# An identity matmul in place of four mask products, in a windowed attention and MLP kernel on one Trainium2 core

## The chip, the cores and the metric

The kernel runs on 1 core of one Trainium2 chip. A core has five engines with an instruction queue each: TensorE (matmul, PE in the views; its weight loads are shown apart as PEld), VectorE (DVE), ScalarE (ACT), GpSimd (POOL) and SyncE (SP). Each engine takes its own instructions strictly in the order in which they are written, and waits where one needs another engine's result or a transfer. SP, ACT and POOL also issue the transfers (DMA) between memory and the core.

The metric is the device time of one execution in microseconds (us), as a median of several runs.

## What is computed

Attention with a causal window of 128 positions plus four "sink" positions that every query sees, and behind it a two-layer MLP with a quick GELU:

```
scores = q @ k.T / sqrt(64)                      # 4 batches, 8 heads, 768 positions, 64 wide
keep   = (key position < 4) | (0 <= query - key < 128)
a      = softmax(where(keep, scores, -1e9))
x      = (a @ v) as 3072 tokens x 512
h      = x @ w_in                                # 512 x 2048
out    = (h * sigmoid(1.702 * h)) @ w_out        # 2048 x 512
```

All inputs and the output are 32-bit floats in memory; the kernel computes in 16-bit floats with 32-bit sums.

## The kernel before

**Blocks.** The 3072 tokens are cut into 12 blocks `k` of 256 tokens, three (`r` = 0, 1, 2) to a batch. A block has four pairs `p` of heads. For each pair: the queries and keys are cast to 16 bits and transposed on TensorE (`tp`, L547) and copied to `qkT`; the scores are multiplied (`s`, L671) into two banks of PSUM, one for each head; ScalarE takes the exp (L700) into `at`; VectorE multiplies `at` by the 0/1 tile `mask` (L710 for `r` > 0, 512 columns a head; L714 for `r` = 0, 384 columns a head); TensorE multiplies by v (`av`, L742 and L747), with a column of ones that gives the sums; VectorE takes the reciprocal (L762) and the product `xn` (L764); TensorE transposes `xn` (`xt`, L775) and a copy gives `xT`. In blocks with `r` > 0 the sink keys come in through a matmul and an exp of their own (`sink`, L576, and L584), from the small tiles `ks16` and `vs16`, into which the first keys and values of the batch are copied (`ks`, L567 by way of L304; `vs`, L470). In blocks 0 and 1 the scores are made one pair at a time, later for two pairs at once, with transposes of other blocks behind them.

**The MLP.** Block k's `xT` is multiplied with `w_in` in eight slabs `s` (`mm1`, L815), each two sums over four parts of 256 columns; ScalarE takes tanh (L829), VectorE joins it to `gT` (L831). The second layer (`mm2`) is plain for block 0 (L993) and takes seven products in place of eight for the others (L892), with sums of operands on VectorE (L862) and partial results added up on VectorE (L919).

**The order.** No loop fixes the order of the instructions. The kernel describes its work as operations with dependences, a cost on each engine that may do it, and a rank (`prio`); a small planner (`Plan.run`) then places them one after the other in a planned time, with planned landings of the transfers, and the instructions of each engine are written in that order. What changes a cost, a rank, a dependence or a choice of engine can therefore reorder every queue after it. The planner also fills TensorE's planned idle time before 12 us with dummy matmuls of `zero` (L1061). Rank and engines are set by constants: `EARLY` shifts a block's attention ahead in eighths of a block's time, `VS_ON`/`VS_AT` and `KS_ON` say which engines may make the `vs` and `ks` copies of batch 0 and when, `LOADS` ranks the first transfers on POOL's queue.

**The loads.** Block 0's queries and keys come in through SP and ACT as 32-bit floats (L497). Block 1's come through SP (L509), in two halves of the heads, and are cast by whichever engine the planner picks (L524). All others, v and the weights are cast on the way by transfers that POOL issues (L426, L450, L386). POOL's queue has eight places: an issue waits until the transfer eight places before has landed. `w_in`'s first two slices of 512 columns come in two halves each.

**The lines that matter here.** The helper `copy` is L304, so every copy and cast of every engine has that line, and tiles tell them apart. `scores` starts at L648, its mask products at L707; `back`, with `av`, at L722; `weights` at L373.

Of the kernel before, what the change touches and what calls it, by code (L numbers as in the profile page):

```python
# [14 lines left out]
P = 128  # L15
# [39 lines left out]
class Plan:  # L55
# [4 lines left out]
    def op(self, eng, dur, lat, fn, deps=(), prio=0.0, acq=None, rel=(), kind=""):  # L60
        return self.any({eng: (dur, lat)}, lambda _: fn(), deps, prio, acq, rel, kind)
# [143 lines left out]
def kernel(  # L205
# [26 lines left out]

    SEVEN_FROM, SEVEN_TO = 1, NK

    EARLY = {1: 5, 2: 5, 3: 0}
    HALVES_FROM, HALVES_X_FROM = 4, 3
    V1_BEHIND = None

# [1 line left out]

    ROUNDED_FROM = 2, 2
    GO1 = None, 1
    VS_ON, VS_AT = "POOL DVE ACT", 15000.0
    QK_NS, V_NS = 1000, 300
    NH = NF // 2
    HM = d_model // 2
# [6 lines left out]

    ident = pool.tile([P, P], FP16, name="ident")
    mask = pool.tile([P, 4 * P], FP16, name="mask")
    dummy = pool.tile([P, 8], FP16, name="dummy")
    zero = pool.tile([P, P], FP16, name="zero")
    w_in16 = pool.tile([P, 4, d_ff], FP16, name="w_in16")
# [26 lines left out]
    def f32(o, i=0):  # L285
        return bank[o.banks[i]]
# [7 lines left out]
    def pick(ns, engs):  # L294
        return {e: ns[e] for e in engs.split()}
# [12 lines left out]
    def uses(name, slot, o):  # L308
        users.setdefault((name, slot), []).append(o)
# [3 lines left out]
        return users.pop((name, slot), [])  # L313

    NEVER = -1e9
    o_zero = op("DVE", 100, 200, lambda: nc.vector.memset(zero, 0.0), prio=NEVER, kind="const")

    def make_ident():
# [20 lines left out]
    o_mask0 = op("POOL", 1900, 1950, make_mask, [o_mask1], prio=NEVER + 1, kind="const")  # L339
    o_mask = op("DVE", 560, 660, keep_sinks, [o_mask0], prio=NEVER + 3.5, kind="const")  # L340

    def ones():
        for t in v16:
            nc.vector.memset(t[:, :, :, D : D + 1], 1.0)
# [17 lines left out]

    COPY = ["DVE ACT"] * NK

    KS_ON = "POOL DVE ACT", "POOL"

    ISSUE = 700
    o_win, o_wout, o_w = {}, {}, []
# [4 lines left out]
    def weights(j, at):  # L373

        if j < 4:
            dst, src = w_in16[:, :, bass.ts(j, 512)], moe_w_in[:, bass.ts(j, 512)]
        else:
            dst, src = w_out16[:, bass.ts(j - 4, 4)], moe_w_out[bass.ts(j - 4, 512), :]

        before = o_w[-3:-2]  # L380
        parts = 2 if j < HALVED else 1
        got = []
        for n in range(parts):
            c = slice(4 * n // parts, 4 * (n + 1) // parts)
            def f(c=c):
                nc.gpsimd.dma_start(dst[:, c], src.rearrange("(c p) f -> p c f", p=P)[:, c])  # L386
            o_l = op("POOL", ISSUE - 150 * (parts - 1), (2600 / parts,), f, before, prio=load_at(f"w{j}b") if n and f"w{j}b" in LOADS else at + 0.1 * n, kind="w")
            loads.append(o_l)
            got += [o_l] * (2 // parts)
        o_w.append(o_l)  # L390
        for n in range(2):
            (o_win if j < 4 else o_wout)[2 * (j % 4) + n] = got if j < 4 else o_l

    L = 16600.0
    LOADS = ["a0", "a1", "v0", "b1", "v1", "w0", "w1", "a2", "w2", "a2", "w3", "v2", "w4", "w6", "w5", "w7"]

    SLABS = (0, 1, 4, 5, 2, 3, 6, 7)

    def load_at(x):
# [128 lines left out]

    k_ap = k

    o_qkT, o_ks, o_se, o_m, o_xT, o_n = {}, {}, {}, {}, {}, {}

    def front(k, p):

# [7 lines left out]
        if k < HALVES_FROM:  # L542
            def tp():
                ps = f16(o_tp).rearrange("d (e j i p) -> d e j i p", e=2, j=2, i=2)
                for i in range(2):
                    for e in range(2):
                        nc.tensor.transpose(  # L547
                            ps[:, e, :, i, :], c16[:, i, e, 2 * p : 2 * p + 2].rearrange("s h d -> s (h d)"), ident
                        )

            if p == 0:
                o_T["war", k] = reuse("qkT", k % RKT)
            war = o_T["war", k]
            o_tp = op("PE", 4 * pe_ns(P), 3 * pe_ns(P) + P / 2.4 + 166, tp,
                      [*o_cqk[k, p], o_ident] + war, prio=base - 5 * h8, acq=("t", 1), kind="tp")
            uses("qk16", k % RQ, o_tp)
            o_cp = plan.any(pick({"DVE": (331, 430), "ACT": (477, 600)}, COPY[k]), lambda e: copy(
                e, T[:, :, :, p].rearrange("d j e s -> d e j s"),
                f16(o_tp).rearrange("d (e j s) -> d e j s", e=2, j=2)),
                [o_tp] + war, prio=base - 5 * h8, rel=[(o_tp, 0)], kind="cp")  # L560
            o_qkT[k, p] = [o_cp]
# [86 lines left out]
    def scores(k, pairs, more=None):  # L648
# [6 lines left out]
        for p in pairs:  # L655
            u = NP * k + p
            o_m["war", k, p] = reuse("at", u % RA)
            deps += [*o_qkT[k, p]] + o_m["war", k, p] + ([*o_qkT[k - 1, p]] if r else [])

        def s():  # L660
            for n, p in enumerate(pairs):
                T, prev = qkT[k % RKT], qkT[(k - 1) % RKT]
                if r:
                    parts = [(prev, 1, PREV, 0, 1), (T, 0, CUR0, 0, 2), (T, 1, CUR1, 1, 2)]
                else:
                    parts = [(T, 0, 0, 0, 2), (T, 1, 2 * P, 1, 2)]
# [13 lines left out]
        if more:  # L680
# [2 lines left out]

            deps += [o_P.get(AHEAD[pairs[0]](k))]
        dur += lead
        o_s = op("PE", dur, dur + 80, s, deps, prio=base - 3 * h8, acq=("s", 2 * len(pairs) + (2 if more else 0)),
                 kind="s")
        if more:
            more[1](o_s, 2 * len(pairs), nominal(k, 0))
# [3 lines left out]
        for n, p in enumerate(pairs):  # L693
# [4 lines left out]
            for i in range(2):  # L698
                def f(n=n, i=i, A=A):
                    nc.scalar.activation(  # L700
                        out=A[:, i, 0:W], in_=f32(o_s, 2 * n + i)[:, 0:W], func=AF.Exp, scale=scale
                    )
                o_e.append(op("ACT", W / 1.2 + 50, W / 1.2 + 170, f, [o_s], prio=base - 2.5 * h8,
                              rel=[(o_s, 2 * n + i)], kind="exp"))
                o_e[-1].lead[o_s] = lead

            def m(A=A, m_=mask):  # L707
                if r:
# [4 lines left out]
                else:  # L713
# [5 lines left out]
            o_m[k, p] = op("DVE", 2 * W / 1.92 + 65, 2 * W / 1.92 + 155, m, o_e + [o_mask],  # L719
                           prio=base - 2 * h8, kind="mask")  # L720

    def back(k, p):  # L722

# [378 lines left out]
```

## Time and profile before

| | us |
|---|---|
| median of 3 runs | 218.59 |
| lowest and highest run | 218.42, 220.57 |
| the profiled execution's own time | 218.56 |
| its span, first to last instruction | 216.9 |
| granted TensorE clock | 1.00 of full speed |

The profile shows the span of one execution; 1.66 us of that execution lie outside its span. Busy time counts instructions that compute; an engine that waits or issues a transfer is not busy. A view's row names the line, the engine, the operation, the tiles it writes and reads (`out<-in`, without buffer numbers) and their shapes; an idle time in square brackets is that of the engine just before the row, and the arrow names what ended it. Rows of equal instructions that follow each other are merged (x2). By engine, the core is busy 211.1 us on TensorE, 187.4 on VectorE, 134.2 on ScalarE and 83.2 on POOL.

### The profile page before, as it was taken

The numbers are of one execution on the slowest core, as the hardware profiler recorded it, in microseconds if no ns is written. First come the engines' busy times: TensorE is split into PE (matmuls) and PEld (weight loads), VectorE is DVE, ScalarE is ACT, GpSimd is POOL, SyncE is SP. The second block draws the span as 40 slices with busy tenths as digits, with TensorE's granted clock in tenths as the row PEclk, the third lists the DMA queues.
The fourth block names the chain that finished last, engine by engine and source line by source line (L and its number), as shares of the span: only waits on it lengthen the run. The fifth ranks groups of instructions, "written<-read, shape, count | busy, mean of one in ns | idle before, by whom it ended". The sixth has DMA issues, their size and how long they took to land.

```text
span 216.9 us, 6618 instructions
## 1 busy us (share of the span) xinstructions
PE 211.1 (97%) x2689; PEld 182.1 (84%) x2689; DVE 187.4 (86%) x435; ACT 134.2 (62%) x276; POOL 83.2 (38%) x134
## 2 busy tenths in 40 slices
PE   7979999999999999999999999999999999999994
PEld 7758887678988988988988889889889889898883
DVE  5898899998988989889889889789879789878674
ACT  3697696365775865755765775854675855744330
POOL 7888564479997090489320080340000000000000
PEclk9999999999999999999999999999999999999999
DMA  6999999999999599099970099091040021022042
GB/s 178 209 193 180 200 192 205 170 163 159 108 165 168 36 125 96 5 116 162 112 124 3 0 103 117 5 105 45 3 94 5 3 68 30 3 53 47 2 100 97
DMA packets 79734, 21.41 MB, mean 99 GB/s; under 512 B 68184, under 2 KB 76888, under 8 KB 79704
## 3 DMA queue, kind: packets, MB, share of 16 engines
q0 software_dynamic: 71200, 12.59, 73.1%
q1 hardware_dynamic: 7416, 7.88, 13.6%
q10 hardware_dynamic: 1088, 0.52, 0.8%
q8 instruction: 21, 0.34, 0.6%
q14 instruction: 9, 0.07, 0.1%
HBM read 27.26 MB, written 6.29 MB: 155 GB/s over the span
## 4 chain that ended last, share of the span: by engine, by line
PE 92%; ACT 3%; DVE 2%; ACTq 1%; issue 0%
PE bank L815 39%; PE bank L892 31%; PE bank L671 5%; PE bank L747 5%; PE bank L993 3%; PE bank L547 2%; PE bank L609 2%; PE bank L742 2%; PE bank L576 2%; ACT at L700 1%; ACTq L497 1%; DVE osb L919 1%; PE bank L1061 1%; PE bank L633 1%; PE bank L775 1%; ACT L360 1%
## 5 line engine op out<-in xcount | busy, mean ns | idle before, releaser
L815 PE MATMUL bank<-xT,w_in 128*128 128x256 f16 x768 | 102.0, 273 | 0.0
L829 ACT ACTIVATE th<-bank 128x512 f16<-128x512 f32 x96 | 57.9, 607 | 55.3 <-PE bank L815 45.9
L815 PEld LDWEIGHTS <-w_in 128*128 128x128 f16 x768 | 72.6, 98 | 8.9
L831 DVE SCALAR_TENSOR_TENSOR gT<-th,bank 128x512 f16<-128x512 f16 x96 | 64.5, 679 | 10.1 <-ACT th L829 10.0
L700 ACT ACTIVATE at<-bank 128x512 f16<-128x512 f32 (+1 forms) x96 | 49.0, 577 | 3.8 <-PE bank L671 3.1
L450 POOL DMA_DIRECT2D v<-in_v_dram x48 | 33.1, 709 | 33.0 <-PE bank L747 26.3
L892 PEld LDWEIGHTS <-sm 128*128 128x128 f16 x352 | 33.2, 98 | 4.2 <-issue 0.2
L892 PE MATMUL bank<-wt,sm 128*128 128x256 f16 x264 | 36.1, 273 | 0.0
L919 DVE SCALAR_TENSOR_TENSOR osb<-bank,osb 128x256 f32<-128x256 f32 x58 | 23.8, 417 | 11.0 <-PE bank L892 10.8
L892 PEld LDWEIGHTS <-gT 128*128 128x128 f16 x264 | 24.9, 98 | 3.2
L892 PE MATMUL bank<-w_out,gT 128*128 128x256 f16 x176 | 26.1, 273 | 0.0
L710 DVE TENSOR_TENSOR at<-at,mask 128x1024 f16<-128x1024 f16 x32 | 21.8, 681 | 0.7 <-ACT at L700 0.6
L764 DVE TENSOR_TENSOR xn<-bank,rcp 128x256 f16<-128x256 f32 x48 | 20.0, 417 | 0.5
L747 PE MATMUL bank<-v,at 128*128 128x65 f16 x352 | 20.1, 193 | 0.0
L426 POOL DMA_DIRECT2D qk<-in_k_dram x20 | 17.7, 900 | 2.5 <-PE bank L815 1.2
L426 POOL DMA_DIRECT2D qk<-in_q_dram x20 | 18.0, 914 | 1.5 <-DMA qk<-in_q_dram 0.5
L747 PEld LDWEIGHTS <-at 128*128 128x128 f16 x352 | 17.4, 98 | 0.9 <-issue 0.2
L862 DVE TENSOR_TENSOR sm<-gT 128x1024 f16<-128x1024 f16 x22 | 15.0, 682 | 0.3
L917 ACT ACTIVATE osb<-bank 128x256 f32<-128x256 f32 x22 | 8.4, 382 | 9.1 <-PE bank L892 9.1
L584 ACT ACTIVATE ats<-bank 128x256 f16<-128x256 f32 x32 | 12.7, 396 | 1.2 <-PE bank L576 1.1
L671 PE MATMUL bank<-qkT 64*128 64x256 f16 x192 | 13.4, 244 | 0.0
L892 PE MATMUL bank<-wt,gT 128*128 128x256 f16 x88 | 13.1, 273 | 0.0
(56 smaller groups left out, 218.2 us busy)
## 6 DMA issues: line engine op xcount, KB each, us to landing
out_dram<-osb SPq DMA_DIRECT2D x48, 128.0 KB
v<-in_v_dram POOLq DMA_DIRECT2D x48, 64.0 KB, 5.0
qk<-in_q_dram POOLq DMA_DIRECT2D x20, 128.0 KB, 5.5
qk<-in_k_dram POOLq DMA_DIRECT2D x20, 128.0 KB, 5.8
w_out<-in_moe_w_out_dram POOLq DMA_DIRECT2D x4, 512.0 KB, 11.4
w_in<-in_moe_w_in_dram POOLq DMA_DIRECT2D x4, 256.0 KB, 7.3
w_in<-in_moe_w_in_dram POOLq DMA_DIRECT2D x2, 512.0 KB, 9.7
qk<-in_k_dram ACTq DMA_DIRECT2D x4, 128.0 KB
```

The source lines that it names most:

```text
L426: nc.gpsimd.dma_start(c16[:, i, e, hs], src[b, hs, t0 : t0 + TB].rearrange("h (p i) d -> i p h d", i=2)[i])
L450: o = op("POOL", ISSUE, (430 if k < 2 else V_NS,), lambda i=i, j=j, src=src: nc.gpsimd.dma_start(w16[64 * i : 64 * i + 64, j, :, 0:D], src ...
L671: nc.tensor.matmul(f32(o_s, 2 * n + i)[:, c : c + w].rearrange("s (j t) -> s j t", t=P), src[d, j, 1, p], T[d, j0:j1, 0, p], start=True, s ...
L700: nc.scalar.activation(out=A[:, i, 0:W], in_=f32(o_s, 2 * n + i)[:, 0:W], func=AF.Exp, scale=scale)
L710: nc.vector.tensor_tensor(out=a_, in0=a_, in1=m_[:, 2 * P :].unsqueeze(1).to_broadcast((P, 4, 2 * P)), op=ALU.mult,)
L747: nc.tensor.matmul(avp()[:, j, i], A[:, i, c : c + P], src[:, jj, 2 * p + i, 0:E], start=not r and n == 0, stop=n == len(blocks) - 1, skip ...
L764: o_nn = op("DVE", 333, 425, lambda: nc.vector.tensor_tensor(out=X[:, p].rearrange("s j (h d) -> s j h d", h=2), in0=avp()[:, :, :, 0:D], ...
L815: nc.tensor.matmul(f32(holder[0])[:, bass.ts(e, TB)], w_in16[:, c, bass.ts(Fi, P)], X[:, c], start=(c == 0 and not (halved and e)), stop=( ...
L829: o_t = op("ACT", 477, 600, lambda first=first: nc.scalar.activation(out=th[first.places[0]], in_=f32(first), func=AF.Tanh, scale=0.851), ...
L831: o_g[k, s] = op("DVE", 595, 690, lambda first=first, s=s: nc.vector.scalar_tensor_tensor(out=g[:, 2 * s : 2 * s + 2].rearrange("p a t -> ...
L892: nc.tensor.matmul(f32(holder[bank_of])[:, 0:HM], x[:, Fi], w[:, Fi], start=first and Fi == 0, stop=Fi == NH - 1, skip_group_check=True)
L919: f, ns = (lambda: nc.vector.scalar_tensor_tensor(out=out, in0=src(), scalar=0.5, in1=add, op0=ALU.mult, op1=ALU.add)), (333, 425)
```

## The change

A second tile, `bias`, is made from `mask` on VectorE: 0 where the mask is 1, and -30000 where it is 0. For the pairs 2 and 3 of block 0 and the pairs 0 and 1 of block 1 the product of `at` with `mask` on VectorE goes. In its place TensorE writes `bias` into each score bank first, by a matmul with the identity (`mb`, two matmuls for a pair, 384 columns each in block 0 and 512 in block 1, ahead of the scores in TensorE's order and dependent on the pair's transposes), and the scores are added to it (`start=False`). The exp then gives 0 where a key is not seen. `av` of these pairs depends on the exps alone.

The other edits are to constants and ranks. Block 1's attention is ranked one eighth of a block later (`EARLY` 5 to 4). The `vs` copies of batch 0 may not go to POOL any more and rank earlier; the `ks` copies of batch 0 may not go to VectorE. The first load of `w_in` is planned with 700 ns less. `av` of every block ranks one eighth of a block earlier. A doubled entry of `LOADS` goes, which moves no load against another.

What the planner makes of it: on TensorE the `mb` pairs stand before 12 us, 72 dummies are left of 89, and `av` moves up by one to three operations in nearly every block. On VectorE four mask products and the four `ks` copies of batch 0 are gone, `bias` is made before the second cast, and all four `vs` copies of batch 0 stand one after the other. ScalarE makes the `ks` copies of pairs 0, 1 and 2 and POOL that of pair 3, ahead of `w_in`'s first issue. The cast of block 1's first half of queries goes from VectorE to ScalarE, that of its second half of queries from POOL to VectorE, that of its second half of keys from ScalarE to POOL, where the loads of block 2 stand behind it. In blocks 4, 5, 7, 8 and 10 the scores of pairs 2 and 3 move up by half a product of the second layer and one operand sum (L862) moves behind the mask of pair 2.

```
-    EARLY = {1: 5, 2: 5, 3: 0}
+    EARLY = {1: 4, 2: 5, 3: 0}
-    VS_ON, VS_AT = "POOL DVE ACT", 15000.0
+    VS_ON, VS_AT = "DVE ACT", 12000.0
...
+    bias = pool.tile([P, 4 * P], FP16, name="bias")
...
+    OUT = -30000.0
+    MASK_AT = 14000.0
+    BIAS = {0: (2, 3), 1: (0, 1)}
...
+    o_bias = op("DVE", 310, 420, lambda: nc.vector.tensor_scalar(
+        out=bias, in0=mask, scalar1=-1.0, scalar2=-OUT, op0=ALU.add, op1=ALU.mult), [o_mask], prio=MASK_AT, kind="mask")
...
-    KS_ON = "POOL DVE ACT", "POOL"
+    KS_ON = "POOL ACT", "POOL"
...
-            o_l = op("POOL", ISSUE - 150 * (parts - 1), (2600 / parts,), f, before, ...)
+            o_l = op("POOL", ISSUE - 150 * (parts - 1), (2600 / parts - (0 if o_w or got else 700),), f, before, ...)
...
-    LOADS = ["a0", "a1", "v0", "b1", "v1", "w0", "w1", "a2", "w2", "a2", "w3", "v2", "w4", "w6", "w5", "w7"]
+    LOADS = ["a0", "a1", "v0", "b1", "v1", "w0", "w1", "a2", "w2", "w3", "v2", "w4", "w6", "w5", "w7"]
...
             o_tp = op("PE", 4 * pe_ns(P), 3 * pe_ns(P) + P / 2.4 + 166, tp, ...)
+            o_tps[k, p] = o_tp
...
+        add, o_b = pairs[0] in BIAS.get(k, ()), None
+        if add:
+            def mb():
+                for i in range(2):
+                    to = f32(o_b, i)[:, 0:W]
+                    if r:
+                        to, m_ = to.rearrange("s (n c) -> s n c", n=2), bias[:, 2 * P :].unsqueeze(1).to_broadcast((P, 2, 2 * P))
+                    else:
+                        m_ = bias[:, 0:W]
+                    nc.tensor.matmul(to, ident, m_, start=True, stop=False, skip_group_check=True)
+
+            o_b = op("PE", 2 * pe_ns(W), 2 * pe_ns(W) + 80, mb, [o_tps[k, pairs[0]], o_bias], prio=base - 4.6 * h8 + 0,
+                     acq=("s", 2), kind="mb")
+            deps.append(o_b)
...
-                            f32(o_s, 2 * n + i)[:, c : c + w].rearrange("s (j t) -> s j t", t=P),
-                            src[d, j, 1, p], T[d, j0:j1, 0, p], start=True, stop=True,
+                            f32(o_b or o_s, 2 * n + i)[:, c : c + w].rearrange("s (j t) -> s j t", t=P),
+                            src[d, j, 1, p], T[d, j0:j1, 0, p], start=not add, stop=True, skip_group_check=add,
...
+            o_m[k, p] = o_e
+            if add:
+                continue
...
-        deps = [o_m[k, p], *o_cv[k]] + ([o_se[k, p], *o_cv[k - 1], *o_vs[b]] if r else [])
+        deps = [*o_m[k, p], *o_cv[k]] + ([o_se[k, p], *o_cv[k - 1], *o_vs[b]] if r else [])
...
-        o_a = op("PE", dur, dur + 166, av, deps, prio=base - 1 * h8, acq=("a", 1), kind="av")
+        o_a = op("PE", dur, dur + 166, av, deps, prio=base - 2 * h8, acq=("a", 1), kind="av")
```

More of the change, by code (lines that the diff above doesn't have):

```diff
@@ L386, in f @@
                 nc.gpsimd.dma_start(dst[:, c], src.rearrange("(c p) f -> p c f", p=P)[:, c])
-            o_l = op("POOL", ISSUE - 150 * (parts - 1), (2600 / parts,), f, before, prio=load_at(f"w{j}b") if n and f"w{j}b" in LOADS else at + 0.1 * n, kind="w")
+            o_l = op("POOL", ISSUE - 150 * (parts - 1), (2600 / parts - (0 if o_w or got else 700),), f, before, prio=load_at(f"w{j}b") if n and f"w{j}b" in LOADS else at + 0.1 * n, kind="w")
             loads.append(o_l)
@@ L529 @@
     k_ap = k
-    o_qkT, o_ks, o_se, o_m, o_xT, o_n = {}, {}, {}, {}, {}, {}
+    o_tps, o_qkT, o_ks, o_se, o_m, o_xT, o_n = {}, {}, {}, {}, {}, {}, {}
     def front(k, p):
@@ L685, in scores @@
         dur += lead
-        o_s = op("PE", dur, dur + 80, s, deps, prio=base - 3 * h8, acq=("s", 2 * len(pairs) + (2 if more else 0)),
+        o_s = op("PE", dur, dur + 80, s, deps, prio=base - 3 * h8, acq=None if add else ("s", 2 * len(pairs) + (2 if more else 0)),
                  kind="s")
@@ L700, in f @@
                     nc.scalar.activation(
-                        out=A[:, i, 0:W], in_=f32(o_s, 2 * n + i)[:, 0:W], func=AF.Exp, scale=scale
+                        out=A[:, i, 0:W], in_=f32(o_b or o_s, 2 * n + i)[:, 0:W], func=AF.Exp, scale=scale
                     )
                 o_e.append(op("ACT", W / 1.2 + 50, W / 1.2 + 170, f, [o_s], prio=base - 2.5 * h8,
-                              rel=[(o_s, 2 * n + i)], kind="exp"))
+                              rel=[(o_b or o_s, 2 * n + i)], kind="exp"))
                 o_e[-1].lead[o_s] = lead
+            o_m[k, p] = o_e
+            if add:
+                continue
             def m(A=A, m_=mask):
@@ L717, in m @@
                     )
-            o_m[k, p] = op("DVE", 2 * W / 1.92 + 65, 2 * W / 1.92 + 155, m, o_e + [o_mask],
-                           prio=base - 2 * h8, kind="mask")
+            o_m[k, p] = [op("DVE", 2 * W / 1.92 + 65, 2 * W / 1.92 + 155, m, o_e + [o_mask],
+                           prio=base - 2 * h8, kind="mask")]
     def back(k, p):
```

## The prediction

> **What bounds the kernel now.** I read the page's busy times and its chain of waits first.
>
> ```profile
> PE 211.1 (97%) x2689; PEld 182.1 (84%) x2689; DVE 187.4 (86%) x435; ACT 134.2 (62%) x276; POOL 83.2 (38%) x134
> PE 92%; ACT 3%; DVE 2%; ACTq 1%; issue 0%
> ```
>
> TensorE is busy 211.1 of 216.9 us and the chain that ended last runs through it for 92%. A shorter stage elsewhere therefore counts only where TensorE waits. The view of waits, TensorE alone (total, times, longest, us), has three such places:
>
> ```profile
> PE bank L775 <- DVE xn L764: 1.1, 1, 1.1
> PE bank L1061 <- DVE zero L316: 1.1, 1, 1.1
> PE bank L547 <- DVE qk L304: 0.2, 1, 0.2
> ```
>
> The busy times by stretch (length, then PE, PEld, DVE, ACT, POOL with counts, granted clock, DMA share, GB/s) say where:
>
> ```profile
> 12.00:15.70 3.70, 2.54 (x45) 1.55 (x42) 3.45 (x13) 3.64 (x9) 3.15 (x5) 1.00 1.67 185
> 18.60:212.50 193.90, 193.90 (x2462) 168.55 (x2461) 170.76 (x377) 121.91 (x249) 67.49 (x105) 1.00 0.86 90
> 212.50:216.90 4.40, 1.21 (x12) 0.84 (x9) 1.67 (x5) 0.00 (x0) 0.00 (x0) 1.00 0.26 89
> ```
>
> From 18.6 to 212.5 us TensorE is busy without a gap; the last 4.4 us are the tail, which the change leaves as it is. So the time is the moment at which TensorE gets into its unbroken run, plus a fixed amount of work, plus any gap that the new order opens. The start, in TensorE's timeline (start, length):
>
> ```profile
> 15.70 0.28 PE L775 MATMUL bank<-ident,xn 128*128 128x128 f16 x2 [1.07 <-DVE xn L764]
> 16.64 0.39 PE L547 MATMUL bank<-ident,qk 128*128 128x128 f16 x4
> 16.86 0.22 PE L742 MATMUL bank<-vs,ats 128*128 128x130 f16 x1
> 17.10 0.28 PE L747 MATMUL bank<-v,at 128*128 128x65 f16 x4
> 17.22 0.27 PE L576 MATMUL bank<-qkT,ks 128*128 128x256 f16 x1
> 17.75 0.28 PE L775 MATMUL bank<-ident,xn 128*128 128x128 f16 x2
> 18.53 0.60 PE L815 MATMUL bank<-xT,w_in 128*128 128x256 f16 x4
> ```
>
> The first product with w_in starts at 18.53, after a gap of 1.07 ahead of 15.70 in which TensorE waited for VectorE's xn. VectorE reached that xn late, because a mask product stood ahead of it in its order:
>
> ```profile
> 14.21 0.68 DVE L710 TENSOR_TENSOR at<-at,mask 128x1024 f16<-128x1024 f16 x1
> 15.21 0.42 DVE L764 TENSOR_TENSOR xn<-bank,rcp 128x256 f16<-128x256 f32 x1
> ```
>
> **VectorE, part by part.** The groups up to 18.6 us (busy, mean ns of one, idle before):
>
> ```profile
> L714 DVE TENSOR_TENSOR at<-at,mask 128x768 f16<-128x768 f16 x4 | 2.2, 552 | 0.1
> L710 DVE TENSOR_TENSOR at<-at,mask 128x1024 f16<-128x1024 f16 x2 | 1.4, 680 | 0.0
> L304 DVE COPY ks<-qkT 64x4 f16<-64x4 f16 x8 | 1.6, 200 | 0.1
> L338 DVE MEMSET mask<- 128x512 f16 x1 | 0.5, 485 | 0.1
> L304 DVE COPY qkT<-bank 128x512 f16<-128x512 f16 x6 | 2.4, 416 | 0.2
> L304 DVE COPY vs<-v 2x260 f16<-2x260 f16 x1 | 0.3, 305 | 0.0
> L360 ACT ACTIVATE dummy<-zero 128x8 f16<-128x8 f16 x1 | 0.2, 209 | 0.0
> L304 ACT COPY vs<-v 2x260 f16<-2x260 f16 x3 | 1.2, 408 | 0.1
> ```
>
> Two masks of block 0 and two of block 1 go: 2 x 0.55 + 2 x 0.68 = 2.46 us. All eight ks copies leave VectorE: 1.6. It gains the bias tile, at most the 0.49 of the memset of that shape, three vs copies, 3 x 0.31, and one qkT copy, 0.42; it gives one cast and takes one. It is thus 2.2 to 2.3 us lighter ahead of the xn that TensorE waited for, and the gap of 1.07 loses its cause. The bias tile stands ahead of casts that are due before 7 us, where TensorE runs dummies; I cost it at nothing, and at 0.49 if they were late. The vs copies wait for block 0's v with block 1's first two qkT copies queued behind them; one stood there before, and the 2.2 us of relief come ahead of it, so I cost this at nothing too, and at the three copies' 0.9 if it came to the path.
>
> ScalarE gets three pairs of ks copies (64x4). Bounds: two of the 128x8 activations, 0.42, to two of its vs copies, 0.82; I take 0.5, since four elements are nearer to eight than to 260. It loses 1.2 of vs copies, one qkT copy and its late cast, and takes an early cast, so it comes out about even. By the Trainium skill (ScalarE: Activation LUTs, Rules for kernel authors: some 0.3 us for each ACTIVATE and 0.83 ns per element) a pair would be 0.6, an estimate, and the sum below would stay. At 0.82 the scores of block 0 come 0.3 to 0.4 later and about 0.2 of the gain goes.
>
> **TensorE.** Eight matmuls of ident and bias come in, four with 384 columns and four with 512. From two pieces of the chain (start, length):
>
> ```profile
> 42.10 0.87 PE bank L815 x8
> 42.97 1.73 PE bank L993 x8
> ```
>
> 256 columns cost 0.109 each and 512 cost 0.216, so 384 cost about 0.163: 4 x 0.163 + 4 x 0.216 = 1.5 us. All stand in the order ahead of 12 us, among the dummies (the built program has 17 dummies fewer), so I cost them at nothing; without that cover, 1.5. The add for block 1's second pair needs a bank that an exp of block 0 frees, and behind it in TensorE's order stand av of block 0 and block 1's first scores; a wait of some 0.2 there lies inside what follows.
>
> **What is late next.** Block 1's second half of keys is cast by ScalarE at 15.43 now; the change hands that cast to POOL.
>
> ```profile
> 15.43 0.62 ACT L304 CAST qk<-qk 128x512 f16<-128x512 f32 x1
> 13.13 0.60 POOL L304 CAST qk<-qk 128x512 f16<-128x512 f32 x1
> 7.26 0.51 SPq L509 DMA_DIRECT2D qk<-in_k_dram  x1
> q1 hardware_dynamic: 1, 0.00, 0.0%
> DMA to landing us min/median/max: 6.9/7.3/7.6
> qk<-in_q_dram POOLq DMA_DIRECT2D x20, 128.0 KB, 5.5
> ```
>
> When those keys land the views do not say. SP issues them at 7.26. SP's queue has one packet left after 13.2 (the fourth line: the queue in the stretch 13.2 to 16), so they land after 13.2, and before 15.43. POOL's qk loads of the same stretch take 6.9 to 7.6 from issue to landing (fifth line); I take 6.9, so 14.2, an estimate. POOL then casts from 14.3 to 14.9, and block 1's third transposes start at 15.0 instead of 15.82.
>
> From there to the product, with pieces of the rows above: transposes 0.39, qkT copy 0.42, sink and score 0.53 (17.22 to 17.75), av of the first pair 0.52 (16.86 to 17.38), reciprocal some 0.2, xn 0.42, transpose 0.11, and five hand-overs of 0.05: 2.8. So 17.8 instead of 18.53, **0.7 us sooner**. Keys at 13.2 would take off at most a few tenths more, since exps and av come next; keys at 15.4 give 19.0, 0.5 later than now.
>
> POOL's added waits: the ks copy of block 0's last pair stands ahead of w_in's first issue, and the cast waits for the keys with block 2's loads, the next w_in and v issues behind it. Those go out about 1.2 us later. They stand in line anyway: 6.9 to 7.6 to land here, against a median of 5.5 on the page, a line of 1.4 to 2.1. I cost this at nothing; without the line, 1.2 on block 2's loads. w_in's first half slice is only *expected* sooner: its transfer stays, and the number moves only the order in which the instructions are written.
>
> The next bound is block 2's v:
>
> ```profile
> 22.50 0.68 POOL L450 DMA_DIRECT2D v<-in_v_dram  x1 [0.26 <-DMA qk<-in_q_dram]
> DMA to landing us min/median/max: 8.4/8.4/8.4
> 31.82 0.22 PE L742 MATMUL bank<-vs,ats 128*128 128x130 f16 x1
> ```
>
> It lands at 22.50 + 8.4 = 30.9 and is first used at 31.82, so at most 0.9 can be gained before TensorE waits for the line of transfers. 0.7 fits.
>
> **The later blocks.** The new rank of av moves products in nearly every block without adding work. I check the tightest, block 4, third pair:
>
> ```profile
> 70.85 0.69 DVE L862 TENSOR_TENSOR sm<-gT 128x1024 f16<-128x1024 f16 x1
> 72.06 0.68 DVE L710 TENSOR_TENSOR at<-at,mask 128x1024 f16<-128x1024 f16 x1
> 71.83 1.04 PE L815 MATMUL bank<-xT,w_in 128*128 128x256 f16 x8
> 73.14 0.22 PE L742 MATMUL bank<-vs,ats 128*128 128x130 f16 x1
> ```
>
> av moves from 73.14 up to the middle of the two products that start at 71.83, to 72.27. The mask it needs ends at 72.74 now; but the sum of 70.85 goes behind it, and the scores go out half a product sooner, so the mask moves up by 0.74, to 72.0. It fits with 0.2 to spare, and I cost it at nothing.
>
> **Sum.** 216.9 - 0.7 = 216.2 of span; the profiled execution took 218.56, 1.66 more than its span, and the median is 0.03 above that: 216.2 + 1.66 + 0.03 = **217.9 us**.
>
> **Rivals.**
> *The keys are late, no gain.* They land between 14.7 and 15.4: 218.4 to 219.1. For it: only bounds are known. Against: 6.9 was the least time of the neighbouring loads. 0.16.
>
> *Slower: the mask does not make av's new turn.* If VectorE is more than 0.2 late there, TensorE stands still in each of the five blocks of this order (4, 5, 7, 8, 10), by at most 72.74 - 72.27, about 0.5: five times that is 2.5, less 0.7, so up to 220.4; half of it, 219.2. For it: VectorE has 88% of the long stretch. Against: the sum that made the mask late is moved away. 0.12.
>
> *The clock goes cold.* With 17 dummies fewer TensorE could be granted a lower clock as the products begin. The rows show 1.00 in the stretch with the 1.07 gap, and the gap that I expect is no longer. Half the clock over 2.5 us of work would lose 2.5: 217.9 + 2.5 = 220.4. By the Trainium skill (TensorE: Matmul & The Clock Gate, Part 1) the clock halves after an idle window of some 3.4 us; by that rule it stays, and the trace agrees. 0.02.
>
> *More than forecast,* by 0.9 or beyond, needs v sooner than its line allows: 0.04.
>
> **Numbers.** My forecast has 0.66. The range reaches from the cap of 0.9 with 0.2 for the spread of runs below the median, 217.4, up to 219.1, which takes in the late keys and half of the slower rival; about 0.1 is left out. By 1% (2.2 us, about the spread of the runs, 218.42 to 220.57): faster 0.02, within 0.93, slower 0.05, from the upper end of the slower rival and the cold clock.
>
> **What would show it.** Right: no gap over 0.3 ahead of an xn transpose, TensorE's gap before 15 us ending on POOL's cast, the first product at 17.6 to 18.0, no TensorE waits past 32 us. Wrong: the product later than 18.3 (keys or scores late), a wait for v at 30.9 (the cap), waits at L747 on masks in blocks 4, 5, 7, 8, 10 (the slower rival), a granted clock below 1.00.

## The result and the profile after

The changed kernel takes 218.41 us, as a median of 22 runs (217.48 to 221.49), against 219.12 (218.41 to 220.64) for the kernel before on the same chip. The ratio is 0.9963, with a 95% interval of 0.9946 to 0.998: 0.4% faster, less than the 1% that the prediction called no change. One of the 22 runs, at 221.49 with a granted clock of 0.99, was in a slow state and is left out of the ratio. The profiled execution took 218.23, with a span of 216.2 in place of 216.9 and a granted clock of 1.00. A second set of runs gave 218.26 against 219.05, ratio 0.9959 (0.9935 to 0.9984).

The view of waits, TensorE alone (total, times, longest, us), no longer has a wait on `xn`:

```profile
PE bank L1089 <- DVE zero L321: 1.1, 1, 1.1
PE bank L555 <- DVE qk L305: 0.6, 2, 0.5
PE bank L585 <- DVE qkT L305: 0.2, 1, 0.2
PE bank L555 <- POOL qk L305: 0.2, 1, 0.2
```

In the changed kernel the copy helper is L305, the transposes `tp` are L555, the identity matmuls `mb` L678, the sinks L585, `xt` L803, `mm1` L843 and the masks L738 and L742. Busy times by stretch (length, then PE, PEld, DVE, ACT, POOL with counts, clock, DMA share, GB/s):

```profile
12.00:15.70 3.70, 3.35 (x57) 2.26 (x55) 3.53 (x14) 2.32 (x7) 2.50 (x4) 1.00 1.64 183
18.60:212.50 193.90, 193.90 (x2462) 168.57 (x2460) 170.69 (x380) 120.21 (x245) 70.49 (x106) 1.00 0.86 89
```

TensorE is busy 0.81 us more between 12 and 15.7 (3.35 against 2.54), and from 18.6 on there is no gap, as before. So the whole difference arises ahead of the first `w_in` product. The timeline there (start, length; in brackets the idle time ahead of the row and what ended it):

```profile
4.63 0.29 DVE L347 TENSOR_SCALAR bias<-mask 128x512 f16<-128x512 f16 x1
...
9.17 0.40 ACT L305 COPY ks<-qkT 64x4 f16<-64x4 f16 x2
...
11.93 0.59 PE L678 MATMUL bank<-bias,ident 128*128 128x512 f16 x2
...
14.40 0.60 POOL L305 CAST qk<-qk 128x512 f16<-128x512 f32 x1 [1.20 <-DMA qk<-in_k_dram]
...
15.06 0.34 PE L555 MATMUL bank<-ident,qk 128*128 128x128 f16 x3 [0.18 <-POOL qk L305]
...
17.91 0.60 PE L843 MATMUL bank<-xT,w_in 128*128 128x256 f16 x4
```

POOL waits 1.20 for block 1's second half of keys and casts them from 14.40; TensorE waits for that cast; the first product starts at 17.91 in place of 18.53. That is 0.62 sooner, and the span is 0.7 shorter.

The view of the chain that ended last (start, length, what) adds something that the waits of TensorE do not show. In the kernel before, the chain to the first product does not run through the `xn` that TensorE waited 1.07 for. It runs through ScalarE, which is busy 3.64 of the 3.70 us from 12 to 15.7: three `vs` copies, the exps, then the cast of block 1's second half of keys, and only then the transposes of these keys on TensorE:

```profile
14.43 0.98 ACT at L700 x2
...
15.43 0.63 ACT qk L304
...
16.10 0.34 PE bank L547 x3
```

In the changed kernel ScalarE is busy 2.32 us in that stretch, since the `vs` copies are on VectorE and the cast is on POOL. The chain now runs through VectorE:

```profile
12.53 0.38 PE bank L775 x12
...
15.17 0.42 DVE xn L792
15.59 0.34 DVE qkT L305
...
15.98 0.28 PE bank L585
```

VectorE starts that `qkT` copy at 15.51; the transposes of the keys that POOL cast end at 15.40 (15.06 + 0.34). So the path by the keys and the path by VectorE's own queue end within about 0.1 us of each other here.

### The profile page after: what moved, and what is told of

Its sections match the earlier page's. It is cut to its first block, busy times and chain, and to the rows that moved or that the text cites. A ratio compares the mean times of both kernels' runs of the same rounds, so it can differ in the third digit from the quotient of the medians.

```text
span 216.2 us, 6592 instructions
## 1 busy us (share of the span) xinstructions
PE 210.8 (97%) x2680; PEld 181.0 (84%) x2680; DVE 185.4 (86%) x429; ACT 133.1 (62%) x277; POOL 86.0 (40%) x136
## 4 chain that ended last, share of the span: by engine, by line
PE 92%; DVE 3%; DMA 2%; ACTq 1%; issue 0%
PE bank L843 39%; PE bank L920 31%; PE bank L695 5%; PE bank L775 5%; PE bank L1021 3%; DMA qk<-in_k_dram 2%; PE bank L618 2%; PE bank L770 2%; PE bank L585 2%; PE bank L555 1%; DVE osb L947 1%; PE bank L642 1%; PE bank L803 1%; ACTq L505 1%; PE bank L678 1%; DVE xn L792 1%
## 5 line engine op out<-in xcount | busy, mean ns | idle before, releaser
L843 PE MATMUL bank<-xT,w_in 128*128 128x256 f16 x768 | 103.7, 273 | 0.0
L843 PEld LDWEIGHTS <-w_in 128*128 128x128 f16 x768 | 71.9, 98 | 8.9
L920 PEld LDWEIGHTS <-gT 128*128 128x128 f16 x264 | 25.5, 98 | 3.4
L738 DVE TENSOR_TENSOR at<-at,mask 128x1024 f16<-128x1024 f16 x30 | 20.5, 683 | 0.2 <-ACT at L724 0.2
L305 POOL COPY ks<-qkT 64x4 f16<-64x4 f16 x26 | 8.1, 313 | 18.6 <-DVE qkT L305 17.6
```

The costliest lines, as they stand in the source:

```text
L738: nc.vector.tensor_tensor(out=a_, in0=a_, in1=m_[:, 2 * P :].unsqueeze(1).to_broadcast((P, 4, 2 * P)), op=ALU.mult,)
L843: nc.tensor.matmul(f32(holder[0])[:, bass.ts(e, TB)], w_in16[:, c, bass.ts(Fi, P)], X[:, c], start=(c == 0 and not (halved and e)), stop=( ...
L920: nc.tensor.matmul(f32(holder[bank_of])[:, 0:HM], x[:, Fi], w[:, Fi], start=first and Fi == 0, stop=Fi == NH - 1, skip_group_check=True)
```

## The experiments

Medians in us, each beside the kernel before in the same set on the same chip. The ratio is not that of the two medians, so where the difference is small its sign can differ:

| kernel | median | before | difference | ratio, 95% interval |
|---|---|---|---|---|
| changed | 218.41 | 219.12 | -0.71 | 0.9963 (0.9946 to 0.9980) |
| changed, again | 218.26 | 219.05 | -0.79 | 0.9959 (0.9935 to 0.9984) |
| without bias, masks back | 218.84 | 218.71 | +0.13 | 0.9996 (0.9973 to 1.0018) |
| bias alone | 218.91 | 218.71 | +0.20 | 0.9992 (0.9969 to 1.0016) |
| ks and vs copies as before | 218.93 | 219.05 | -0.12 | 0.9981 (0.9959 to 1.0002) |
| av's rank as before | 218.13 | 218.71 | -0.58 | 0.9966 (0.9946 to 0.9985) |
| without the 700 ns | 218.55 | 218.71 | -0.16 | 0.9995 (0.9971 to 1.0018) |
| the same, again | 218.37 | 219.05 | -0.68 | 0.9963 (0.9940 to 0.9986) |
| mb of 8 columns | 218.11 | 218.63 | -0.52 | 0.9974 (0.9945 to 1.0003) |
| bias for all pairs of block 1 | 219.06 | 218.63 | +0.43 | 1.0016 (0.9997 to 1.0034) |
| no gate for block 1's second halves | 219.69 | 219.05 | +0.64 | 1.0023 (0.9995 to 1.0051) |
| block 1's v later by one copy | 218.00 | 218.63 | -0.63 | 0.9958 (0.9932 to 0.9984) |
| by two copies | 218.74 | 218.63 | +0.11 | 1.0025 (1.0001 to 1.0049) |

### Which part brings it: the masks or the copies?

The changed kernel with the four mask products back:

```
-    BIAS = {0: (2, 3), 1: (0, 1)}
+    BIAS = {}
```

> The four mask products are back on VectorE (the table of pairs is empty, so no mb matmul is issued); every other edit of the change stays. Theory, the four mask products that leave VectorE are what brings the first w_in product from 18.53 to 17.91: it starts at 18.1 to 18.5 here, again with a wait of TensorE on VectorE's xn of 0.3 to 1.1 before 18 us, and the span is 0.3 to 0.7 longer than the changed kernel's 216.2. Rival, the constants (which engines make the ks and vs copies, block 1's rank, which engine casts) bring it: the first product stays at 17.8 to 18.0 and the span within 0.15 of 216.2.

Its timeline shows a mask of block 1 ahead of an `xn` on VectorE, and TensorE's wait for that `xn`:

```profile
15.24 0.68 DVE L738 TENSOR_TENSOR at<-at,mask 128x1024 f16<-128x1024 f16 x1
15.84 0.42 DVE L792 TENSOR_TENSOR xn<-bank,rcp 128x256 f16<-128x256 f32 x1
...
16.32 0.29 PE L803 MATMUL bank<-ident,xn 128*128 128x128 f16 x2 [0.57 <-DVE xn L792]
```

TensorE waits as in the kernel before, and the median is the kernel before's. The span of 217.2 is 1.0 longer than the changed kernel's, and the product, at 18.61, is later than expected too. The rival falls: the constants alone show no gain.

The bias alone, all other edits undone:

```
-    EARLY = {1: 4, 2: 5, 3: 0}
+    EARLY = {1: 5, 2: 5, 3: 0}
-    VS_ON, VS_AT = "DVE ACT", 12000.0
+    VS_ON, VS_AT = "POOL DVE ACT", 15000.0
-    KS_ON = "POOL ACT", "POOL"
+    KS_ON = "POOL DVE ACT", "POOL"
...   (and the 700 ns and av's rank as before)
```

> The bias tile and the mb matmuls alone; block 1's rank, the engines of the ks and vs copies, the 700 ns and the rank of av as in the kernel before. Theory, relief of VectorE alone does it: the first w_in product starts at 17.7 to 18.1, and the span is within 0.4 of the changed kernel's 216.2, what is longer being a wait of TensorE of up to 0.4 between 20 and 32 us that the order of the first blocks opens. Rival, the constants are needed for the gain at the start: the first product at 18.3 or later, span 216.7 or more with no wait after 18 us.

Here the theory falls too. Four masks fewer on VectorE, and the median is at +0.20. In its profiled execution (219.52, slower than its median by 0.6) the cast of keys that POOL makes in the changed kernel stands on VectorE behind block 0's `xn`, and TensorE waits for it and then for the next `xn`:

```profile
15.23 0.65 DVE L305 CAST qk<-qk 128x512 f16<-128x512 f32 x1
...
15.94 0.56 PE L555 MATMUL bank<-ident,qk 128*128 128x128 f16 x7 [0.24 <-DVE qk L305]
16.68 0.29 PE L803 MATMUL bank<-ident,xn 128*128 128x128 f16 x2 [0.18 <-DVE xn L792]
...
19.02 0.60 PE L843 MATMUL bank<-xT,w_in 128*128 128x256 f16 x4
```

The rival's numbers for the start hold (product past 18.3, span 217.7), though a small wait of 0.13 between 29 and 29.5 is there as well. The planner had given the free time on VectorE to other work: the eight `ks` copies stay there, and both second-half casts come. The chain of this execution runs through two of these copies and the cast behind them (10.97 to 11.83) as well. So the third kernel has everything but the engines of the `ks` and `vs` copies:

```
-    VS_ON, VS_AT = "DVE ACT", 12000.0
+    VS_ON, VS_AT = "POOL DVE ACT", 15000.0
-    KS_ON = "POOL ACT", "POOL"
+    KS_ON = "POOL DVE ACT", "POOL"
```

> The changed kernel with the engines of the ks and vs copies of batch 0, and the vs copies' rank, as in the kernel before; bias, block 1's rank, the 700 ns and av's rank stay. Theory, VectorE's load ahead of 16 us is what counts, and the ks copies on VectorE (8 of 0.2) are as much a part of it as the masks: the first product 0.3 to 1.1 later than the changed kernel's 17.91, a wait of TensorE on a copy, cast or xn of VectorE between 14 and 17 us, median 0.2 to 0.8 above the changed kernel's. Rival, what the run with the bias alone lacked was block 1's rank and the 700 ns: then this kernel is within 0.15 of the changed one.

Its median is 0.67 above the changed kernel's of the same set, as the theory said. The `ks` copies stand ahead of a cast on VectorE, and TensorE waits for the cast:

```profile
10.38 0.33 DVE L305 COPY ks<-qkT 64x4 f16<-64x4 f16 x2
10.74 0.63 DVE L305 CAST qk<-qk 128x512 f16<-128x512 f32 x1
...
11.43 0.34 PE L555 MATMUL bank<-ident,qk 128*128 128x128 f16 x3 [0.31 <-DVE qk L305]
...
18.12 0.60 PE L843 MATMUL bank<-xT,w_in 128*128 128x256 f16 x4
```

Its product starts only 0.2 after the changed kernel's 17.91, though, less than the 0.3 to 1.1 that was expected; a wait of 0.13 between 28 and 28.5 us is added to it, and the span is 216.8. By the medians, each against its own kernel before: with only the masks off VectorE -0.12, with only the copies off it +0.13, neither of which can be told from no change; with both -0.71 and -0.79. So neither part alone shows a gain, though for the masks alone the interval still allows up to 0.9 us. No run gives back to ScalarE alone its `vs` copies and its late cast, so what their leaving brings by itself is not shown.

### Does av's rank cost anything?

```
-        o_a = op("PE", dur, dur + 166, av, deps, prio=base - 2 * h8, acq=("a", 1), kind="av")
+        o_a = op("PE", dur, dur + 166, av, deps, prio=base - 1 * h8, acq=("a", 1), kind="av")
```

> The changed kernel with av's rank as in the kernel before. Theory, av's earlier rank costs and brings nothing (it was priced at nothing, with 0.2 to spare at the tightest place): span 216.1 to 216.4, no wait of TensorE past 18 us, first product at 17.8 to 18.0. Rival 1, the earlier rank opens waits in blocks 4, 5, 7, 8 and 10 that the trace of the changed kernel hides in longer products: the span is 0.3 or more shorter here. Rival 2, the earlier rank is itself part of the gain: 0.3 or more longer.

The median is 0.58 below the kernel before, the span 216.4, the product at 18.04, and TensorE does not wait past 18 us. The product is 0.04 later than the theory's bound; both rivals asked for 0.3 of span and do not show, as far as one span, and a median 0.1 to 0.2 short of the changed kernel's, can tell. The order differs in one more point, however: POOL makes no cast here, and both casts of block 1's second halves stand on VectorE. The later one is this:

```profile
14.46 0.41 DVE L305 CAST qk<-qk 128x512 f16<-128x512 f32 x1
```

So the gain does not hang on POOL as the engine of that cast, nor is a cast on VectorE by itself what loses it in the kernel with the bias alone.

### Does the number at w_in's first load cost anything?

```
-... (2600 / parts - (0 if o_w or got else 700),) ...
+... (2600 / parts,) ...
```

> The changed kernel with w_in's first half slice expected as late as in the kernel before; transfers and their issues are the same ones. Theory of the prediction, the number moves only the order in which instructions are written and is worth nothing: first product at 17.8 to 18.0, span 216.0 to 216.4, no wait of TensorE from 18 to 32 us. Rival, that order matters: TensorE finds operations written in a turn for which their banks or inputs are not yet free, with waits of 0.2 to 0.6 in all between 22 and 28 us, and a span of 216.4 to 216.8.

The median of -0.16 and the span of 216.6, with 0.13 of waits at 27.5 to 28.5, looked like the rival. Since the intervals overlapped, the same kernel was run again beside the changed one:

> The changed kernel with w_in's first half slice expected as late as before, once more, beside the changed kernel. The first runs of it, on another day's set, lay 0.16 below the kernel before, the changed kernel's 0.71. Theory A, the order that the 700 ns give is worth 0.2 to 0.5: median 0.2 to 0.5 above the changed kernel's of this set, with a wait of TensorE of about 0.1 at 27.5 to 28.5 in the profile again. Theory B (the prediction's), it is worth nothing and the difference was the spread of the runs: medians within 0.15.

> The changed kernel itself, once more, so that the other kernels of this set stand beside it on the same chip: 0.4 to 1.0 below the kernel before in the median, first w_in product at 17.8 to 18.1, span 216.0 to 216.4.

Now the two medians are 218.37 and 218.26, within the 0.15 of theory B. That does not settle it: two medians of 12 runs each cannot tell 0.1 from a few tenths, and theory A's sign is there again. TensorE waits 0.13 (at 27.0 to 27.5), as in the first execution, while neither execution of the changed kernel has a wait there. From the first product to the end of the span are 198.7 and 198.6 us without the 700 ns and 198.3 both times with them, so their order seems to be worth about 0.3 behind the first product. The medians neither confirm nor exclude this. Ahead of the first product something else decides, as the profiled executions of this set show. The changed kernel again, and then the kernel without the 700 ns:

```profile
14.61 0.60 POOL L305 CAST qk<-qk 128x512 f16<-128x512 f32 x1 [1.57 <-DMA qk<-in_k_dram]
...
18.06 0.60 PE L843 MATMUL bank<-xT,w_in 128*128 128x256 f16 x4
```

```profile
13.33 0.60 POOL L305 CAST qk<-qk 128x512 f16<-128x512 f32 x1 [0.65 <-DMA qk<-in_k_dram]
...
17.13 0.60 PE L843 MATMUL bank<-xT,w_in 128*128 128x256 f16 x4
```

In the second the cast is 1.3 us sooner, the product 0.9 sooner, and the span is 215.7. The first profiled execution of that same kernel cast the keys at 14.48 and had its product at 17.93. The order did not do that, since the kernel is the same: the transfers landed sooner.

### Do the identity matmuls cost anything?

Their width cut to 8 columns, with the order of all engines kept, and four more of them where there are no dummies:

```
-                    nc.tensor.matmul(to, ident, m_, start=True, stop=False, ...)
+                    nc.tensor.matmul(f32(o_b, i)[:, 0:8], ident, bias[:, 0:8], start=True, stop=True, ...)
```

> The changed kernel in its own order, instruction for instruction, but each of the eight mb matmuls writes 8 columns in place of 384 or 512, and the scores start their sums anew; so the mask of these four pairs is left out of the computation. Theory of the prediction, the mb matmuls lie among dummies and waits and cost nothing: median and span within 0.2 of the changed kernel's (0.7 to 0.8 below the kernel before), first product at 17.7 to 18.1. Rival, they hold up the chain ahead of 16 us: their 1.5 us of TensorE comes back in part, first product 0.3 or more sooner at the same landing of the keys, median 0.3 to 1.0 below the changed kernel's.

```
-    BIAS = {0: (2, 3), 1: (0, 1)}
+    BIAS = {0: (2, 3), 1: (0, 1, 2, 3)}
```

> The changed kernel with the other two pairs of block 1 done by the identity matmul too: four more mb matmuls of 512 columns, which stand in TensorE's order behind the dummies, between 14 and 19 us, and two mask products of 0.68 fewer on VectorE there. Theory, without the cover of the dummies an mb matmul costs what it takes: 4 x 0.216 = 0.86 more on TensorE, of which at most 0.3 falls into its wait for POOL's cast, and VectorE's two products were not on the path; median 0.5 to 0.9 above the changed kernel's, so about as slow as the kernel before. Rival, VectorE is still what holds TensorE up at this place: median equal to the changed kernel's or lower.

With 8 columns the median is 0.52 below the kernel before, no lower than the changed kernel's -0.71 and -0.79 of other sets. The gain of the rival does not show; with an interval from -1.2 to +0.1 us, a few tenths are not excluded. The profiled execution (219.00, 0.9 above the median) was one with late keys:

```profile
15.42 0.60 POOL L305 CAST qk<-qk 128x512 f16<-128x512 f32 x1 [1.60 <-DMA qk<-in_k_dram]
...
18.88 0.60 PE L843 MATMUL bank<-xT,w_in 128*128 128x256 f16 x4
```

From the cast to the product are 3.46 us, against 3.51 (17.91 - 14.40) and 3.45 (18.06 - 14.61) with full width. That confirms the length of this chain; the price of the `mb` matmuls it cannot show, because all of them stand ahead of the cast. For that, look at what stands behind them. Dummies stand behind block 0's pairs, but the last dummies start at 10.15 and block 1's pairs at 11.28 and 11.93, behind all of them. In the changed kernel VectorE, which takes over from TensorE there, shows no wait in its timeline from 9.28 to 16.4, so an earlier `av` would have found it busy: they cost next to nothing. In the execution with the soonest loads (cast at 13.33) VectorE does wait for the `av` behind these pairs:

```profile
11.25 0.59 PE L678 MATMUL bank<-bias,ident 128*128 128x512 f16 x2
...
12.13 0.18 DVE L790 RECIPROCAL rcp<-bank 128x4 f32<-128x4 f32 x1 [0.19 <-PE bank L775]
```

There they can cost up to 0.2.

With four more the median is 0.43 above the kernel before, which is 1.1 to 1.2 above the changed kernel, more than the 0.5 to 0.9 expected. TensorE's timeline:

```profile
15.46 0.59 PE L678 MATMUL bank<-bias,ident 128*128 128x512 f16 x2
15.89 0.39 PE L555 MATMUL bank<-ident,qk 128*128 128x128 f16 x4
...
17.48 0.59 PE L678 MATMUL bank<-bias,ident 128*128 128x512 f16 x2
17.98 0.29 PE L803 MATMUL bank<-ident,xn 128*128 128x128 f16 x2
...
19.18 0.61 PE L843 MATMUL bank<-xT,w_in 128*128 128x256 f16 x4
```

The next operation follows the first pair after 0.43, 0.215 for each matmul, and the second after 0.50. The chain of this execution runs from POOL's cast at 14.51 through both pairs, 0.43 each, so 0.86 of the loss is theirs. In this order two `av` of the second pair also stand ahead of the first product, so 19.18 is not a clean measure of it; a wait of 0.08 at 31 is added. The rest of the 1.1 was not taken further. The rival falls: the chain from the cast to the product passes nothing on VectorE.

### Are the keys what is late next?

First the gate away that keeps SP from issuing block 1's second halves before block 0's v; all other instructions stay in their order:

```
-    GO1 = None, 1
+    GO1 = None, None
```

> The changed kernel without the gate (a 1x1 memset of POOL behind block 0's v loads) that holds back SP's two issues of block 1's second halves; all other instructions and their order stay. SP then issues them at about 4.6 and 5.0 in place of 6.85 and 7.27. Theory of the prediction, these keys are what is late next behind the xn: they land 0.5 to 2 sooner, POOL casts them sooner, TensorE's wait ahead of 15.1 on POOL's cast goes, and the first product comes 0.1 to 0.4 sooner, the median 0.1 to 0.4 below the changed kernel's. Rival, the transfers share one line, and what the keys gain, block 0's and block 1's v lose: vs copies and av later, first product at 17.9 or later, median the same or up to 0.5 above.

The theory falls, and the rival's direction holds: +0.64 on the kernel before, and 1.4 above the changed kernel of the same set, more than the 0.5 that the rival allowed. SP issues the second halves at 5.52 and 5.93, later than expected but 1.2 sooner than in the changed kernel. From the timeline of its profiled execution, which at 218.59 is one of its fastest, 1.1 below the median:

```profile
13.10 0.45 PE L775 MATMUL bank<-v,at 128*128 128x65 f16 x9 [0.55 <-DMA v<-in_v_dram]
...
13.34 0.70 POOL L394 DMA_DIRECT2D w_in<-in_moe_w_in_dram  x1 [0.78 <-DMA v<-in_v_dram]
14.10 0.89 POOL L305 CAST qk<-qk 128x512 f16<-128x512 f32 x1
...
18.46 0.60 PE L843 MATMUL bank<-xT,w_in 128*128 128x256 f16 x4
```

SP's keys went out ahead of half of block 0's v, and now that v is late: `av` waits 0.55 for it, and POOL, whose queue waits for v too, casts the keys at 14.10 with no wait for the keys themselves. By the Trainium skill (DMA: Bandwidth & Descriptors, Issuing engines are not separate DMA queues) transfers issued from different engines run on the same 16 DMA engines and interleave. This run agrees: two issues of SP, 1.2 us sooner, made POOL's v late. What the slower executions lose beyond this one, no profile shows.

Then the line in the other direction: block 1's v, which is needed later, is held back on POOL by one or two copies of a 128x512 tile to a spare tile. All else stays in its order:

```
+   op("POOL", 10, 20, lambda: copy("POOL", idle, mask), [o_mask], prio=load_at("v1") - 0.2, kind="go")
    (once or twice, ahead of block 1's v issues)
```

> The changed kernel with one copy of a 128x512 tile to a spare tile on POOL (some 0.5 to 0.9) ahead of block 1's four v issues; every other instruction in the same order. SP's issues of block 1's second halves then stand ahead of more of that v in the line of transfers. Theory, the keys' landing sets the first product, and the line is one for all: keys land 0.2 to 0.7 sooner, block 1's v not later than 15.5 (used at 16.5), first product as much sooner as the keys, median 0.1 to 0.5 below the changed kernel's. Rival 1, the transfers of the two kinds do not stand in one line, keys land as before, nothing changes. Rival 2, POOL's later issues of w_in and block 2 or block 2's v (30.65, used at 31.2) take the gain back: product sooner, but a wait of TensorE between 27 and 33, and the same median.

> As the kernel with one copy, with two (1.0 to 1.8 later). Theory: keys land 0.5 to 1.3 sooner than in the changed kernel, at 13.0 to 13.8; first product 17.2 to 17.6, median 0.3 to 0.8 below the changed kernel's, with block 2's v as the next wait (0.1 to 0.4 at about 31). Rivals as there; and a third, POOL's ks copy of block 0's last pair comes late behind the issues, and block 1's scores with it: product at 18 or later.

With one copy, and with two:

```profile
13.79 0.60 POOL L305 CAST qk<-qk 128x512 f16<-128x512 f32 x1 [0.27 <-DMA qk<-in_k_dram]
...
17.71 0.49 PE L843 MATMUL bank<-xT,w_in 128*128 128x256 f16 x3
```

```profile
11.40 2.83 POOL L394 DMA_DIRECT2D w_in<-in_moe_w_in_dram  x4
14.28 0.60 POOL L305 CAST qk<-qk 128x512 f16<-128x512 f32 x1
...
17.90 0.60 PE L843 MATMUL bank<-xT,w_in 128*128 128x256 f16 x4
```

With one copy the cast is 0.61 sooner than in the changed kernel's first execution and the product only 0.20 sooner: the chain here runs through VectorE's `vs` copies and `xn`, and not through the keys, and TensorE waits 0.2 each on a cast and an `xn` of VectorE. Whether the copy brought the keys sooner is not shown, since the cast of the same keys moved by more than that between two executions of one kernel (14.48 and 13.33). The median, -0.63, is the changed kernel's within the spread: no better version. With two copies POOL itself is late: it issues `w_in` until 14.23 and casts at 14.28 with no wait for the keys, and the chain runs through these issues. The product is at 17.90 and the span 216.5, but this execution, 218.42, is the fastest of its 12; the median is at +0.11, and by the ratio the kernel is slower than the kernel before. What the slower executions wait for is not shown. The third rival named POOL, but for this execution the wrong operation on it: the cast and not the `ks` copy.

## Why the prediction was right

- *VectorE's relief removes the 1.07 wait on `xn`*: right, there is none. The prediction added masks and copies up in one sum; the runs show that it takes both. With either half alone no gain shows: in the one order a mask stays ahead of the `xn`, in the others `ks` copies stand ahead of a cast. The wait was not the whole cause of the late product, however. The chain of the kernel before ran through ScalarE's `vs` copies, exps and cast at 15.43, so with the wait gone and the cast left where it was, the transposes at 16.10 would, by that chain, not have moved. The prediction has that cast only in its next step, where the change hands it to POOL; it takes both steps.
- *What is late next is block 1's second half of keys, by POOL's cast from 14.3, and a chain that ends at 17.8*: cast at 14.40, product at 17.91. The length from cast to product, 3.5 in the prediction, was 3.45 to 3.51 in four executions that waited for the keys (14.40, 14.48, 14.61, 15.42). In the two with the later keys the chain does run from their landing. In the other two it runs through VectorE, which is done about as late; this second path the prediction did not add up. The landing itself was an estimate from the least of the neighbouring loads, and with casts between 13.33 and 15.42 in the traces, meeting it to 0.1 us in the first execution is partly luck. The gain of 0.7 came out as 0.62 at the product and 0.7 in the span.
- *Keys at 13.2 would take off a few tenths at most*: so it was with the cast at 13.79 (0.61 sooner gave 0.20). With the cast at 13.33 it was 0.8 (17.13), but there the work of block 0 was ahead as well: its first `av` begins at 11.68 in place of 12.37.
- *`mb` costs nothing among dummies and 0.216 for 512 columns without them*: 0.215 measured where nothing covers them. Only block 0's pairs have dummies behind them; block 1's were covered by VectorE's queue, and can cost up to 0.2 when the loads come soonest.
- *The small terms*: the bias tile took 0.29 (bound 0.49). A pair of `ks` copies on ScalarE took 0.40, where 0.5 was taken and 0.42 was the lower bound; no step hung on it. By the Trainium skill (ScalarE: Activation LUTs, Rules for kernel authors), whose figure is for an ACTIVATE, the estimate for the pair was 0.6; for these copies of four elements that is too high, and the measurement decides.
- *The later blocks*: the tightest place came out as worked out, 0.62 sooner than in the old clock.

```profile
70.72 0.68 DVE L738 TENSOR_TENSOR at<-at,mask 128x1024 f16<-128x1024 f16 x1
...
71.65 0.68 DVE L890 TENSOR_TENSOR sm<-gT 128x1024 f16<-128x1024 f16 x1
71.66 0.22 PE L770 MATMUL bank<-vs,ats 128*128 128x130 f16 x1
```

  The mask ends at 71.40 (forecast 72.0 - 0.62) and `av` starts at 71.66 (forecast 72.27 - 0.62): 0.26 to spare. The slower rival fell there, and av's rank put back changed nothing that its median shows.
- *w_in expected sooner moves only the order*: right for the first product. The order itself was given no price; by the two profiled executions it may be worth 0.3 behind the first product, which the medians (0.55 and 0.11) leave open.
- *Block 2's v caps the gain at 0.9*: not seen. The cap took the issue of that v as fixed at 22.50; in the execution with the product at 17.13, 1.4 sooner than before, its last part went out at 21.74 and TensorE did not wait for it.
- *The number*: 218.41 is 0.5 above the 217.9 forecast and inside the range. The 0.5 is the level of the set, in which the kernel before took 219.12 and not the 218.59 that the sum started from; the difference of -0.7 is the one forecast. The 217.4 to 219.1 of the range was more than the change itself; the difference beside the kernel before is the better test.

## What to carry to other kernels

Work taken off an engine ahead of a wait counts only if nothing else is put in its place: with a planner, read the built order and not the sum of durations, and expect that two halves of a relief may each show no gain. Read the chain beside the waits: the longest wait of the busiest engine need not lie on it. Behind the wait that goes, look for the transfer that lands next and add up the chain from its landing, and do the same for the queue of each engine that feeds it; here two such paths ended within 0.1 us. Issuing one transfer 1.2 us sooner made another one late here, and with two more copies on the engine that issues no gain was left.

## What was not expected of the hardware

Most of the spread between profiled executions arises ahead of the first product. In five executions of three kernels (the changed one, the one without the 700 ns, the one with 8 columns) SP issues block 1's second halves at the same times within 0.15 us. POOL's cast of these keys began, after a wait for them, between 13.33 and 15.42, and the span went with it: 215.7 at 13.33, 216.2 at 14.40, 216.6 at 14.48, 216.4 at 14.61, 217.2 at 15.42. That is 1.5 us, twice what the change is worth, so a single profile of each of two such kernels can show either one to be the faster. Why the same transfers take longer in one execution than in another, no run shows.
